# Turning the Fourier mixer's folded tokens by VectorE and DRAM instead of by TensorE

## The chip, the cores and the metric

The kernel runs on one core of a Trainium2 chip. The metric is the device time of one execution in microseconds (us); lower is better.

## What is computed

Three blocks follow each other on 2 batches of 3136 tokens with 256 features; all tensors are float32. The first is an attention with squared ReLU scores and a gate, the second a low-rank token mixer with an MLP, the third a Fourier mixer with a normalised MLP:

```python
out = u * (np.maximum(z @ z.T / S, 0.0) ** 2 @ v)      # attention, S = 3136
x   = out + (out.T @ U @ V).T                          # low-rank mixer
x   = x + np.maximum(x @ w_ch1, 0.0) @ w_ch2           # MLP, 256 -> 1024 -> 256
m   = np.real(fft(fft(x, axis=1), axis=2))             # Fourier mixer
y   = x + m
yn  = (y - mean(y)) / sqrt(var(y) + 1e-06)
res = y + np.maximum(yn @ w_ch1b, 0.0) @ w_ch2b        # second MLP
```

Matmuls take each float32 operand as a high and a low part (`h` and `l`, the low one being the value minus the high one), and do three products of four.

## The kernel before

**Stages.** Attention fills the first 549 us. Then 28 chunks of 448 tokens go through the two MLPs: 14 of layer 1 (7 for each batch), then 14 of layer 2. A chunk takes 8 steps, so that there are 224 steps, numbered here by the loop counter `i` of the last loop of `program` (lines 1091 to 1120). A plain step is 12 matmuls of 448 columns on TensorE (PE): six of `hidden(k)` for step i (L337 to L339) and six of `project` for step i-2 (L362 to L364). ScalarE (ACT) and VectorE (DVE) turn the hidden values into `Hh` (L342) and `Hl` (L343), which `project` needs two steps later.

**Work beside the steps.** After its 12 matmuls a step advances the generators in the list `active` by one piece each, and writes their instructions behind it on every engine. The newest chunk's preparation (`prep1`, `prep2`) stands first in the list, then the conversion of the second MLP's weights, then `fourier(b)`. Every engine executes its instructions in the order in which they were written. `fourier(0)` starts at step 50 and `fourier(1)` at step 106; both are skipped in steps whose number divides by 8 (56 and 112 here).

**The Fourier mixer's first half.** The mixer of a batch works on 8 groups of 4 x 98 tokens. Features come in pairs of halves that are folded: `fold(i)` adds them on DVE (L875, three sums, six for the first group) into a tile `y` with features on the partitions and 392 tokens in the free dimension. `tokens(i)` turns it token-major: four TensorE transposes of 98 tokens each (L886) into one PSUM bank, from which ACT makes `nh` (a copy, L93) and DVE `nl` (a difference, L96). `axis49(i)` applies the 49-point transform, three matmuls of 512 columns (L893 to L895), copies the result to `wst` on ACT and stores it into the DRAM tensor `scr` from SyncE (SP), L902. `pair_late()` hands out the pairs of `nh` and `nl`, of which there are two. In one step stand `fold(i)`, `tokens(i-1)` and `axis49(i-2)`, so that a group is folded in one step, turned in the next and transformed in the one after it. The two batches have 16 groups.

**After that** the mixer reads `scr` back (`fetch`, L938), applies the 64-point transform and the feature transform, and adds the result to `xT`.

**Queues.** `load` issues a DMA from SP, `late_dma` from GpSimd (POOL). SP issues in order: a DMA that waits for its data or its buffer holds up all that stand behind it. In the first half of the mixer SP's queue holds the stores into `scr` and a few of the weight conversion.

## Time and profile before

| | |
|---|---|
| time, median of 3 runs | 1165.17 us (1165.17 to 1165.97) |
| the profiled execution | 1166.43 us |
| its span, first to last instruction | 1164.7 us |
| PE busy | 1150.9 us (99%), 8438 matmuls |
| DVE busy | 853.5 us (73%) |
| ACT busy | 645.7 us (55%) |
| POOL busy | 141.7 us (12%) |
| TensorE clock granted, mean | 0.999 |
| DMA | 78.72 MB, 68 GB/s over the span |

Busy time counts an engine as busy while at least one of its instructions runs; matmuls overlap in the pipeline, so the length of a PE record (0.36 us for 448 columns) is longer than the distance from one start to the next. Distances between starts tell what an instruction costs.

### The profile page before, as it was taken

Reading aid. Unit: us, or ns where it says so; the run is one execution under the profiler, and the core shown is the slowest. Engines: PE = TensorE matmul, PEld = TensorE weight load, DVE = VectorE, ACT = ScalarE, POOL = GpSimd, SP = SyncE. Lnnn points to the kernel's source line nnn. Section 1 sums busy time; section 2 is a strip of 40 time slices with the busy share of each in tenths; the row PEclk is TensorE's granted clock in tenths of the full one; section 3 lists DMA queues with packets and bytes.
Section 4 is the critical chain, followed back from the end, with each engine's and each line's share of the span. In section 5 each row is a group of like instructions: output and inputs, shape, how many; then the busy total and the mean of one; then the engine's idle time right before and its main releaser. Section 6 shows DMA issues by size and latency. Waiting matters only on the chain.

```text
span 1164.7 us, 21602 instructions
## 1 busy us (share of the span) xinstructions
PE 1150.9 (99%) x8438; PEld 1075.7 (92%) x8438; DVE 853.5 (73%) x1599; ACT 645.7 (55%) x1061; POOL 141.7 (12%) x236
## 2 busy tenths in 40 slices
PE   9999999999999999999999999999999999999998
PEld 8999999999988999998999989999989999999997
DVE  6877888778888777777577674566487788767674
ACT  7867777777777666665354344333264443434342
POOL 0012320122012201220201000110000110000010
PEclk9999999999999999999999999999999999999999
DMA  4322222324222211221533322111012211110111
GB/s 140 95 59 63 77 86 61 97 74 129 68 53 92 73 40 57 74 78 43 172 98 118 107 86 75 28 33 55 1 46 69 49 48 40 32 40 26 40 32 48
DMA packets 64454, 78.72 MB, mean 68 GB/s; under 512 B 13150, under 2 KB 55008, under 8 KB 64352
## 3 DMA queue, kind: packets, MB, share of 16 engines
q1 hardware_dynamic: 53088, 56.98, 15.7%
q0 software_dynamic: 10848, 20.16, 6.7%
q8 instruction: 66, 1.08, 0.4%
q14 instruction: 36, 0.29, 0.1%
q10 hardware_dynamic: 416, 0.20, 0.1%
HBM read 51.89 MB, written 25.34 MB: 66 GB/s over the span
## 4 chain that ended last, share of the span: by engine, by line
PE 88%; DVE 7%; ACT 3%; issue 2%; DMA 1%; DVEq 0%; ACTq 0%; SPq 0%
PE psO L567 31%; PE psS L536 8%; PE psH L337 7%; PE psH L338 7%; PE psH L339 7%; PE psC L362 7%; PE psC L364 7%; PE psC L363 7%; DVE l L96 1%; ACT P L542 1%; ACT P L545 1%; DVE h L546 1%; DMA vraw<-in_v 1%; DVE Hl L343 1%; PE ps_g L840 1%
## 5 line engine op out<-in xcount | busy, mean ns | idle before, releaser
L567 PE MATMUL psO<-h,Vt 64*128 64x448 f32 x2744 | 347.4, 363 | 2.5 <-DVE h L546 1.5
L567 PEld LDWEIGHTS psO<-h,Vt 64*128 64x128 f32 x2744 | 294.5, 185 | 14.7 <-DVE h L546 2.6
L96 DVE TENSOR_TENSOR l<-P,h 128x896 fp32r<-128x896 f32 (+2 forms) x239 | 226.1, 951 | 33.7 <-ACT h L93 16.5
L343 DVE SCALAR_TENSOR_TENSOR Hl<-psH,Hh 128x448 fp32r<-128x448 f32 x224 | 139.0, 623 | 141.2 <-ACT Hh L342 139.9
L342 ACT ACTIVATE Hh<-psH 128x448 fp32r<-128x448 f32 x224 | 120.3, 541 | 203.9 <-PE psH L339 198.9
L567 PE MATMUL psO<-l,Vt 64*128 64x448 f32 x1372 | 209.5, 363 | 0.2
L542 ACT ACTIVATE P<-psS 128x896 f32<-128x896 f32 (+1 forms) x183 | 161.2, 882 | 66.5 <-PE psS L536 65.1
L545 ACT ACTIVATE P<-P 128x896 f32<-128x896 f32 (+1 forms) x183 | 168.5, 921 | 5.7
L337 PE MATMUL psH<-h,w 128*128 128x448 f32 x448 | 167.1, 373 | 0.0
L567 PEld LDWEIGHTS psO<-l,Vt 64*128 64x128 f32 x1372 | 161.4, 185 | 5.8 <-DVE l L96 1.2
L546 DVE CAST h<-P 128x896 fp32r<-128x896 f32 (+1 forms) x183 | 110.8, 606 | 75.4 <-ACT P L545 73.4
L338 PE MATMUL psH<-l,w 128*128 128x448 f32 x448 | 164.3, 367 | 0.0
L339 PE MATMUL psH<-h,w 128*128 128x448 f32 x448 | 163.9, 366 | 0.0
L362 PE MATMUL psC<-Hh,w 128*128 128x448 f32 x448 | 163.6, 365 | 0.0
L364 PE MATMUL psC<-Hh,w 128*128 128x448 f32 x448 | 163.4, 365 | 0.0
L363 PE MATMUL psC<-Hl,w 128*128 128x448 f32 x448 | 162.4, 362 | 0.0
L536 PE MATMUL psS<-Q,KT 64*128 64x448 f32 x1002 | 149.5, 364 | 3.6 <-DVE G L652 3.1
L536 PEld LDWEIGHTS psS<-Q,KT 64*128 64x128 f32 x1002 | 114.9, 185 | 8.7 <-DVE G L652 4.4
L337 PEld LDWEIGHTS psH<-h,w 128*128 128x128 f32 x448 | 84.3, 188 | 7.7 <-ACT P L93 0.3
L339 PEld LDWEIGHTS psH<-h,w 128*128 128x128 f32 x448 | 84.2, 188 | 7.2
L363 PEld LDWEIGHTS psC<-Hl,w 128*128 128x128 f32 x448 | 84.1, 188 | 7.1 <-DVE Hl L343 0.4
L364 PEld LDWEIGHTS psC<-Hh,w 128*128 128x128 f32 x448 | 84.1, 188 | 6.8
(302 smaller groups left out, 1201.1 us busy)
## 6 DMA issues: line engine op xcount, KB each, us to landing
uT<-in_uT SPq DMA_DIRECT2D x14, 448.0 KB, 3.9
vraw<-in_v SPq DMA_DIRECT2D x24, 256.0 KB, 2.8
out<-P SPq DMA_DIRECT2D x27, 224.0 KB, 1.9
aTd<-aT POOLq DMA_DIRECT2D x13, 448.0 KB, 2.9
aNd<-aT POOLq DMA_DIRECT2D x104, 56.0 KB, 2.4
xT<-aTd SPq DMA_DIRECT2D x6, 896.0 KB, 4.7
scr<-wst SPq DMA_DIRECT2D x16, 256.0 KB, 2.0
Vs<-Vd POOLq DMA_DIRECT2D x28, 112.0 KB, 2.5
```

The source lines that it names most:

```text
L96: tt(out=o, in0=a, in1=b, op=ALU.subtract)
L337: mm(ps[:, 0:CH], wh, self.h[:, a], start=a == 0, stop=False)
L338: mm(ps[:, 0:CH], wh, self.l[:, a], start=False, stop=False)
L339: mm(ps[:, 0:CH], wl, self.h[:, a], start=False, stop=a == 1)
L343: stt(out=l, in0=ps[:, 0:CH], scalar=0.0, in1=f(h), op0=ALU.max, op1=ALU.subtract)
L362: mm(dst, wh, h, start=k == 0, stop=False)
L363: mm(dst, wh, l, start=False, stop=False)
L364: mm(dst, wl, h, start=False, stop=k == 7)
L536: mm(ps[:, j, 0:w], k, q[r, kq, o : o + w], start=(kk, kq) == (0, 0), stop=kk == 1)
L542: act(out=dst, in_=ps[:, j : j + m, 0:w], func=AF.Relu, scale=1.0 / S)
L545: act(out=A[:, x], in_=A[:, x], func=AF.Square)
L567: mm(o[fa][i][:, 0:CH], vt[r, j, k, fa * 128 : fa * 128 + 128], x[r, j * CH : j * CH + CH], start=p == 0 and fa not in [t[1][0] for t in t ...
```

## The change

`fold(i)` now writes into one of two fixed tiles `ys`, padded from 392 to 416 tokens (13 blocks of 32; the padding is zeroed once by GpSimd). DVE turns it in blocks of 32x32 (`STREAM_TRANSPOSE`, L887), into a tile `yt` that shares its buffer with `A1` or `A2` of the mixer's second half. Each band of 32 features is then stored from SP into a new DRAM tensor `nat_d`, token-major, in pieces of 32 features (128 bytes): four DMAs of 52 KB a group (L889). `fetch_tokens(i)` reads 392 token rows of 128 features back from SP into the `nl` tile of a pair (196 KB, L896), and `tokens(i)` makes `nh` from it on ACT and `nl` in place on DVE. A third pair of `nh` and `nl` lies in the tile `Uhl`, which the low-rank mixer no longer needs then. In one step stand `fold(i)`, `fetch_tokens(i-2)`, `tokens(i-3)` and `axis49(i-4)`. The mixer's first half takes 12 pieces instead of 11 (ten, of which the first took two steps). The scratch tiles `sm` grow from four to five.

```diff
+    nat_d = [dram.tile([8, 416, 128], F32, tag=f"natd{b}", name=f"natd{b}") for b in range(NB)]
...
+    ys = [mp.tile([128, 416], F32, tag=f"y{k}", name=f"y{k}", bufs=1) for k in range(2)]
+    for t in (raw128, col128, *(f(r) for r in rows), *(y[:, 392:416] for y in ys)):
         nc.gpsimd.memset(t, 0.0)
...
-        for x in (*nats[0], *nats[1]):
+        uu = Uhl.rearrange("p k h n -> p (k h n)")
+        nats.append([uu[:, 0:512], uu[:, 512:1024]])
+        for x in (*nats[0], *nats[1], *nats[2]):
             nc.gpsimd.memset(f(x)[96:128], 0.0)
...
+            yt = mp.tile([128, 416], F32, tag=f"A{i % 2 + 1}", name="yt", bufs=1)
+            nc.vector.transpose(out=yt, in_=y)
+            for c in (0, 32, 64, 96):
+                load(
+                    out=nat_d[b][i, :, c : c + 32].rearrange("(j t) d -> t j d", t=32),
+                    in_=yt[c : c + 32].rearrange("p (j d) -> p j d", d=32),
+                )
+
+        def fetch_tokens(i):
+            h, l = nat[i] = pair_late()
+            load(
+                out=f(l)[0:98].rearrange("p (s d) -> p s d", s=4),
+                in_=nat_d[b][i, 0:392].rearrange("(s p) d -> p s d", p=98),
+            )
+
         def tokens(i):
-            y = folded.pop(i)
-            ps = misc()
-            for s in range(4):
-                nc.tensor.transpose(ps[0:98, s * 128 : s * 128 + 128], y[:, s * 98 : s * 98 + 98], ident)
-            h, l = pair_late()
-            hcopy(h[0:98], ps[0:98, :])
-            sub(l[0:98], ps[0:98, :], f(h[0:98]))
-            nat[i] = (h, l)
+            h, l = nat[i]
+            hcopy(h[0:98], f(l)[0:98])
+            sub(l[0:98], f(l)[0:98], f(h[0:98]))
...
-        for i in range(10):
+        for i in range(12):
             if i < 8:
                 fold(i)
-            if 0 < i < 9:
-                tokens(i - 1)
-            if i == 0:
-                yield
+            if 1 < i < 10:
+                fetch_tokens(i - 2)
+            if 2 < i < 11:
+                tokens(i - 3)
...
-            if i > 1:
-                axis49(i - 2)
+            if i > 3:
+                axis49(i - 4)
             yield
```

**On PE**, in `fourier(0)`, around the first transform (`ps_x`, `ps_g`, `ps_m` are PSUM banks, `psH` and `psC` those of the MLP). Before:

```order
L257 MATMUL ps_m<-Vs,Gs_87 128x448
L886 MATMUL ps_x<-ident,y 98x128 x4
L893 MATMUL ps_g<-nh_7998,b49h 128x512
L894 MATMUL ps_g<-nl_7999,b49h 128x512
L895 MATMUL ps_g<-nh_7998,b49l 128x512
L337 MATMUL psH<-h,w 128x448
```

and with the change, behind the last matmuls of `project` in step 54:

```order
L364 MATMUL psC_9281<-Hl,w 128x448
L365 MATMUL psC_9281<-Hh,w 128x448
L907 MATMUL ps_m<-nh_8004,b49h 128x512
L908 MATMUL ps_m<-nl_8005,b49h 128x512
L909 MATMUL ps_m<-nh_8004,b49l 128x512
L338 MATMUL psH<-h,w 128x448
```

The transposes are gone, and the first transform stands one step later than before, in step 54 instead of 53.

**On SP**, from the first store of `fourier(0)` on. Before:

```order
L902 DMA scr_70<-wst 128x512 x2
L1063 DMA w2bd<-Tl 128x256
L902 DMA scr_70<-wst 128x512 x3
L927 DMA raw_7988<-xT_7986 32x1x98
L902 DMA scr_70<-wst 128x512 x3
```

and with the change, from the first fold of `fourier(0)` on (`nl_8005`, `nl_8003` and `Uhl` are the three pairs' `nl`):

```order
L889 DMA natd_72<-yt 32x13x32 x12
L896 DMA nl_8005<-natd_72 98x4x128
L1077 DMA w2bd<-Th 128x256
L889 DMA natd_72<-yt 32x13x32 x4
L896 DMA nl_8003<-natd_72 98x4x128
L889 DMA natd_72<-yt 32x13x32 x4
L896 DMA Uhl<-natd_72 98x4x128
L916 DMA scr_70<-wst 128x512
```

Each read-back stands behind the four stores of the group that is folded in the same step: that of group 0 behind those of group 2.

**On DVE**, in `fourier(0)`, the end of step 52 and step 53. Before (`P` and `l` are of the chunk's preparation):

```order
L875 TENSOR_TENSOR y<-xT_7986 128x4x48 x2
L96 TENSOR_TENSOR nl_7999<-ps_g,nh_7998 98x512
L343 SCALAR_TENSOR_TENSOR Hl<-psH,Hh 128x448
L258 TENSOR_TENSOR P<-ps_m,xT_7987 128x448
L96 TENSOR_TENSOR l<-P,h 128x448
```

and with the change:

```order
L887 STREAM_TRANSPOSE yt<-y_7994 128x416
L344 SCALAR_TENSOR_TENSOR Hl<-psH,Hh 128x448
L259 TENSOR_TENSOR P<-ps_g,xT_7989 128x448
L96 TENSOR_TENSOR l<-P,h 128x448
L879 TENSOR_TENSOR y_7995<-xT_7988 128x4x2
L879 TENSOR_TENSOR y_7995<-xT_7988 128x4x48 x2
L887 STREAM_TRANSPOSE yt<-y_7995 128x416
L96 TENSOR_TENSOR nl_8005<-nl_8005,nh_8004 98x512
```

The turn of group 2 now ends the work of step 52, and the first `nl` stands in step 53, behind the fold and the turn of group 3.

## Rows read from the trace of the kernel before

**Rows 1.** The page, parts 1 and 4: busy time, and the chain's shares.

```profile
PE 1150.9 (99%) x8438; PEld 1075.7 (92%) x8438; DVE 853.5 (73%) x1599; ACT 645.7 (55%) x1061; POOL 141.7 (12%) x236
...
PE 88%; DVE 7%; ACT 3%; issue 2%; DMA 1%; DVEq 0%; ACTq 0%; SPq 0%
```

**Rows 2.** Line L886, the transposes: idle of their engine until y came (us, times).

```profile
  DVE y L875: 2.7, 3
```

**Rows 3.** Timeline of PE (start, length, instruction): step 57 and the next one's start.

```profile
700.91 0.36 PE L337 MATMUL psH<-h,w 128*128 128x448 f32 x1
...
703.34 0.60 PE L886 MATMUL ps_x<-ident,y 128*98 128x128 f32 x4
...
704.24 0.39 PE L895 MATMUL ps_g<-nh,b49l 128*128 128x512 f32 x1
704.47 0.36 PE L337 MATMUL psH<-h,w 128*128 128x448 f32 x1
```

**Rows 4.** Timeline of PE: starts of steps 52, 108, 113, 114, and late transposes in step 53.

```profile
682.86 0.37 PE L337 MATMUL psH<-h,w 128*128 128x448 f32 x1
...
689.80 0.64 PE L886 MATMUL ps_x<-ident,y 128*98 128x128 f32 x4 [1.04 <-DVE y L875]
...
845.58 0.37 PE L337 MATMUL psH<-h,w 128*128 128x448 f32 x1
...
861.79 0.36 PE L337 MATMUL psH<-h,w 128*128 128x448 f32 x1
...
865.56 0.36 PE L337 MATMUL psH<-h,w 128*128 128x448 f32 x1
```

**Rows 5.** Timeline of DVE: folds in steps 52, 57, 108, 113, 114, and neighbours.

```profile
689.05 0.69 DVE L875 TENSOR_TENSOR y<-xT 128x8 f32<-128x8 f32 x3
689.66 0.68 DVE L96 TENSOR_TENSOR nl<-ps_g,nh 98x512 fp32r<-98x512 f32 x1
...
704.50 0.70 DVE L875 TENSOR_TENSOR y<-xT 128x8 f32<-128x8 f32 x3
...
848.43 1.15 DVE L96 TENSOR_TENSOR P<-xT,ps_x 128x448 f32<-128x448 f32 x2 [0.15 <-PE ps_x L291]
...
849.83 0.70 DVE L875 TENSOR_TENSOR y<-xT 128x8 f32<-128x8 f32 x3
...
866.31 0.70 DVE L875 TENSOR_TENSOR y<-xT 128x8 f32<-128x8 f32 x3
...
871.59 0.70 DVE L875 TENSOR_TENSOR y<-xT 128x8 f32<-128x8 f32 x3
```

**Rows 6.** DVE's block turns there are: line L604 (nanoseconds), and the timeline.

```profile
L604 DVE STREAM_TRANSPOSE aT<-aT x13: 1103/1105/1111, 55.3 to 516.2; 128x896 f32<-128x896 f32 x13
...
729.68 0.20 DVE L916 STREAM_TRANSPOSE col<-wst 128x32 f32<-128x32 f32 x1
```

**Rows 7.** SP's timeline: four issues in a row; DMA view: KB each, us to landing.

```profile
737.02 1.71 SPq L938 DMA_DIRECT2D wr<-scr  x4
...
aNd<-aT POOLq DMA_DIRECT2D x104, 56.0 KB, 2.4
...
wst<-aNd SPq DMA_DIRECT2D x12, 256.0 KB, 2.7
...
wst<-aNd SPq DMA_DIRECT2D x1, 128.0 KB, 2.0
```

**Rows 8.** Timeline of ACT: the copy that makes nh.

```profile
703.97 0.59 ACT L93 CAST nh<-ps_x 98x512 fp32r<-98x512 f32 x1 [1.10 <-PE ps_x L886]
```

**Rows 9.** Windows: busy us of PE, PEld, DVE, ACT, POOL; clock; two fourier stretches, the end.

```profile
682.86:718.66 35.80, 34.76 (x181) 30.79 (x180) 23.53 (x57) 16.47 (x31) 1.28 (x3) 1.00 0.19 67
845.58:880.63 35.05, 34.57 (x180) 30.48 (x179) 29.72 (x79) 21.23 (x42) 1.10 (x2) 1.00 0.15 54
...
1160.00:1161.00 1.00, 0.19 (x1) 0.00 (x0) 1.00 (x4) 0.00 (x0) 0.00 (x0) 1.00 0.00 0
...
1163.00:1163.50 0.50, 0.00 (x0) 0.00 (x0) 0.00 (x0) 0.00 (x0) 0.00 (x0) 0.91 0.00 0
```

More of the change, by code (lines that the diff above doesn't have):

```diff
@@ L800, in program @@
     rows = [mp.tile([128, CH], F32R, tag=f"row{k}", name=f"row{k}", bufs=1) for k in range(2)]
-    for t in (raw128, col128, *(f(r) for r in rows)):
+    ys = [mp.tile([128, 416], F32, tag=f"y{k}", name=f"y{k}", bufs=1) for k in range(2)]
+    for t in (raw128, col128, *(f(r) for r in rows), *(y[:, 392:416] for y in ys)):
         nc.gpsimd.memset(t, 0.0)
     def small(dt=F32):
-        return mp.tile([128, CH], dt, tag="sm", name="sm", bufs=4)
+        return mp.tile([128, CH], dt, tag="sm", name="sm", bufs=5)
     late["small"] = small
@@ L854, in fourier @@
     def fourier(b):
-        folded, nat, W = {}, {}, {}
+        nat, W = {}, {}
         x0, x1 = (xT[b][:, a].rearrange("p (s m r) -> p s m r", m=49, r=2) for a in range(2))
         def fold(i):
-            y = folded[i] = mp.tile([128, 392], F32, tag="y", name="y")
+            y = ys[i % 2]
             s0, s1 = 4 * i, 4 * i + 4
-            yv = y.rearrange("p (s m r) -> p s m r", m=49, r=2)
+            yv = y[:, 0:392].rearrange("p (s m r) -> p s m r", m=49, r=2)
             for t0, t1 in ((0, 1), (1, s1)) if s0 == 0 else ((s0, s1),):
```

## The prediction

> **What bounds the kernel now.** First the page's busy times and the chain that ended last: PE is busy 99% of the span and holds 88% of the chain, DVE 7% [rows 1]. PE therefore sets the end, and a change is worth what it takes from PE's queue, less what it makes PE wait. Next the windows of the two stretches in which the mixer's first half runs, steps 52 to 61 and 108 to 117: in 35.8 and 35.1 us PE has no more than 1.0 and 0.5 us in which nothing runs, while DVE is busy 23.5 and 29.7 us [rows 9]. Then PE's timeline in one step. Step 57 starts at 700.91, its 12 matmuls fill 2.43 us, four transposes and three transform matmuls fill 1.13 us, and the next step starts at 704.47; a transform matmul takes 0.23 us from its start to the next one's [rows 3]. So a step is 2.43 us plain, 3.12 us with a transform (2.43 + 0.69), 3.56 us with the transposes too, and 0.20 us more where the preparation puts a matmul of 448 columns into it (a twelfth of 2.43). Last the waits at the transposes: PE's side stood idle 2.7 us in three places until DVE had folded y [rows 2], the longest 1.04 us in step 53 [rows 4]. The profiled execution took 1166.43 us, 1164.7 of span and 1.73 around it, which is 1.26 us (0.1%) above the median of the runs. I make the sum as a difference and put it on the median, 1165.17.
>
> **What goes from PE.** Four transposes cost 1.13 - 0.69 = 0.44 us of a step [rows 3]. There are 16 groups, so PE's queue loses 16 x 0.44 = 7.0 us. The waits for y go with them, up to 2.7 us [rows 2]. Gain 9.7 us, all on the path. The price of a transpose is settled by the row: 0.11 us each in this stream. The Trainium skill (VectorE: DVE Perf Modes, "The three transpose paths") gives TensorE 390 ns and VectorE 311 ns for a 128x128 block of 2-byte numbers, and its rules for kernel authors prefer TensorE where PSUM may be the destination. By that figure the 64 transposes would be worth 25 us and the gain 28; the pitch in the trace is less than a third of it, and the sum goes by the trace.
>
> **What is added to DVE.** One block turn a group. The trace has two sizes, 1.105 us for 896 columns and 0.20 us for 32 [rows 6]; the line through both gives 0.20 + 384 x 1.047 ns = 0.60 us for 416. Sixteen are 9.7 us, in stretches where DVE has 12.3 and 5.3 us free [rows 9]. As busy time they fit. The difference that makes nl reads SBUF instead of PSUM; I leave it at 0.68 us [rows 5], and the copy for nh at 0.59 us [rows 8]. The zeroing of padding and of Uhl is GpSimd's, which issues little then; the fifth sm tile costs nothing on any queue.
>
> **What is added to SP and where it leads.** A group now takes four stores and one read-back, five DMAs more in a step. Four issues in a row for 32 partitions each took 1.71 us [rows 7]. A read of 196 KB from DRAM lies between two rows, 2.0 us to landing for 128 KB and 2.7 us for 256 KB [rows 7]; I take 2.4. Bandwidth is no concern: DMA engines are busy 15 to 19% there [rows 9]. The order is. The program's order puts the read-back of group g-2 behind the four stores of group g, which wait for DVE's turn of group g, and DVE turns it at the end of what that step gives it. From the fold's start to the point where the transform has both halves of group g-2 the chain is: fold 0.61 (689.05 to 689.66) [rows 5], turn 0.60, four issues 1.71, landing 2.4, nh 0.59, nl 0.68, together 6.6 us. The transform stands on PE two steps after the fold's step, behind that step's 12 matmuls. It can start 0.23 us before nl is there, with the matmul that needs nh alone. With the lag from the start of a step on PE to its fold on DVE,
>
> PE's wait = lag + 6.6 - 0.23 - 2.43 - (the two steps) = lag + 3.94 - (the two steps).
>
> Behind the waiting transform stand the hidden matmuls of the next step, and so the whole of ACT's and DVE's work for it: nothing fills the gap. The lags, read from the trace of before:
>
> In fourier(0), step 52 starts at 682.86 [rows 4] and its fold at 689.05 [rows 5], because the preparation's copies and the weight conversion lie ahead of it. Lag 6.19. The two steps hold no transform yet, only 2.63 each. Wait 6.19 + 3.94 - 5.26 = 4.9 us in step 54. In step 57 a layer-1 chunk's end lies ahead of the fold: 704.50 - 700.91 = 3.59 [rows 3, 5], two steps of 3.12, wait 1.3 us in step 59. The groups between are covered by the first wait and by step 56, which the mixer skips; the last two read-backs stand behind no fold.
>
> In fourier(1), step 108 starts at 845.58 and the fold in it at 849.83 [rows 4, 5], lag 4.25. DVE is full there, with 0.15 us idle ahead of that row's preparation [rows 5], and the change puts a fold and two turns more ahead of it (0.61 + 1.20), so the lag becomes 5.9. The two steps take 2.63 and 2.43. Wait 4.8 us in step 110. Step 113: 866.31 - 861.79 = 4.52, steps of 3.32 and 3.12, wait 2.0 us. Step 114: 871.59 - 865.56 = 6.03, steps of 3.12 and 3.12 + 2.0, wait 1.7 us [rows 4, 5].
>
> Waits 4.9 + 1.3 + 4.8 + 2.0 + 1.7 = 14.7 us, against a gain of 9.7: plus 5.0 us.
>
> **The clock during the two long waits.** At the end of the program PE runs its last matmul at 1160.0 to 1160.2, and the granted clock, 1.00 until 1163.0, is 0.91 on average from there to 1163.5 [rows 9]: it falls from 2.4 to 1.2 GHz some three us after PE had nothing left. Two waits of almost 5 us lie within the reach of that. At the low level the matmuls take twice as long. No row shows a fall amid work, so I bound it: nothing if the clock stays, one whole step of 3.12 us more for each wait if it stays low over the step that follows. I take 1 us each, nearer to nothing, since PE had work until shortly before the clock could fall: plus 2.0 us. The Trainium skill (TensorE: Matmul & The Clock Gate, "Why this matters for your kernels") warns of idle gaps between bursts of matmuls, which bring the low level back; the end of this trace agrees with it, and by that rule the clock would fall in both waits, which is rival (c) below.
>
> Sum: 5.0 + 2.0 = 7.0 us, 1165.17 + 7.0 = 1172.2, and 1173.4 for an execution profiled as the one before. I predict 1172 us.
>
> **Bounds of the chain.** Low: landing 2.0, and stores issued in 0.3 us less, 5.9 in all, takes 0.7 from each of five waits, 3.5 us. High: landing 2.7, and the read-back held up behind the four stores in the same queue. Stores in pieces of 128 bytes are in the trace from GpSimd's queue alone, 2.4 us to landing for 56 KB [rows 7]; I allow 0.7 us for four from SP. That is 7.6 in all, 5 us more. With the clock at 0 to 6.2 us the forecast's mechanism spans plus 1.5 to plus 16 us, 1167 to 1181.
>
> **Rivals.** (a) The read-back is hidden and the 9.7 us are kept: 1155.5 us. For it speaks that DVE has the free time, and that the lag may shrink once DVE no longer stands behind copies from PE's transposes. Against it: in step 52 the budget from the fold to the transform is 2 x 2.63 + 2.43 + 0.23 - 6.19 = 1.7 us, less than the landing alone. It needs folds that start 5 us earlier than in the rows, or the first two waits to halve and the rest to vanish. (b) Only the first transform of each batch waits, with the short chain: 4.2 + 4.1 us against 9.7, and lesser waits of 1 or 2 us: about 1165, within 0.2%. For it: the later lags are read from a kernel in which PE itself waited. (c) The clock falls in both long waits and stays low for a step or more, on top of stores that hold up the read-back: 1176 to 1181. It decides if the clock falls within the waits as it did at the end of the program [rows 9]. That the change leaves transposes in the queue is no case: none of L886 stands in the new order of PE.
>
> **How the numbers follow.** Forecast 1167.5 to 1176: 0.46. Rival (c), 1176 to 1181 and a little beyond: 0.22. Rival (b), 1163 to 1167.5: 0.17. Rival (a) and its parts, 1155 to 1163: 0.15. About 0.2% (2.3 us) is what a measurement of this kernel tells from no change, so slower 0.68, same 0.17, faster 0.15. The range leaves out most of (a) and the far end of (c): 1161 to 1181.
>
> **What the changed profile would show.** Right: line L886 gone; L907 or L908 with an idle time of 4 to 5 us before it near 690 us and again near 851 us, released by ACT's nh or DVE's nl, and on ACT the nh copies waiting for a DMA into nl; SP's read-backs starting some 1.7 us after the first store of the same step; L887 at about 0.60 us; steps 55 to 61 without waits near 3.12 us. Wrong: PE's first transform with a wait below 2 us, which would mean that the folds come earlier than in the rows; a read-back that lands within 1.5 us; or PE's steps between the waits longer than 3.12 us, which would point at the clock or at Hh and Hl coming late.

## The result, and the profile after the change

The changed kernel takes 1180.64 us (median of 4 runs, 1179.66 to 1181.75) against 1165.56 us before (1165.17 to 1165.97): a ratio of 1.0129, with a 95% interval of 1.0113 to 1.0144. It is slower by 15.1 us; the forecast was 7.0. The sign was right, the size was not. The profiled execution took 1181.75 us, with a span of 1180.0.

The page after the change: part 1, the row of the clock from part 2, and the lines of part 4 (compare [rows 1]):

```profile
PE 1151.9 (98%) x8374; PEld 1064.3 (90%) x8374; DVE 863.8 (73%) x1615; ACT 645.3 (55%) x1061; POOL 143.0 (12%) x240
...
PEclk9999999999999999999999989999989999999999
...
PE psO L568 30%; PE psS L537 8%; PE psH L338 7%; PE psH L340 7%; PE psH L339 7%; PE psC L363 7%; PE psC L364 7%; PE psC L365 7%; DVE l L96 1%; DVE h L547 1%; ACT P L546 1%; ACT P L543 1%; DMA nl<-natd 1%; DMA zraw<-in_zT 1%; SPq L889 1%
```

PE has 64 instructions fewer and is busy 1.0 us longer. Two slices of the clock's row fall below 9, which are the two Fourier stretches, and the chain that ended last now runs through the read-back (`DMA nl<-natd`) and the four stores (`SPq L889`).

The timeline of PE shows what the transform waits for. Below are the instructions with a wait in front of them (in brackets: idle us, and what ended it), and a few behind the first:

```profile
695.56 0.79 PE L907 MATMUL ps_m<-nh,b49h 128*128 128x512 f32 x1 [5.27 <-ACT nh L93]
...
697.30 0.57 PE L338 MATMUL psH<-h,w 128*128 128x448 f32 x1
697.68 0.57 PE L339 MATMUL psH<-l,w 128*128 128x448 f32 x1
...
702.00 0.36 PE L338 MATMUL psH<-h,w 128*128 128x448 f32 x1
702.21 0.36 PE L339 MATMUL psH<-l,w 128*128 128x448 f32 x1
...
711.03 0.50 PE L908 MATMUL ps_m<-nl,b49h 128*128 128x512 f32 x1 [0.38 <-DVE nl L96]
715.93 0.50 PE L907 MATMUL ps_x<-nh,b49h 128*128 128x512 f32 x1 [1.75 <-ACT nh L93]
...
865.52 0.80 PE L907 MATMUL ps_m<-nh,b49h 128*128 128x512 f32 x1 [4.83 <-ACT nh L93]
...
881.00 0.50 PE L907 MATMUL ps_x<-nh,b49h 128*128 128x512 f32 x1 [0.39 <-ACT nh L93]
...
886.20 0.50 PE L907 MATMUL ps_g<-nh,b49h 128*128 128x512 f32 x1 [1.32 <-ACT nh L93]
...
891.13 0.49 PE L907 MATMUL ps_x<-Uhl,b49h 128*128 128x512 f32 x1 [0.84 <-ACT Uhl L93]
...
910.30 0.28 PE L907 MATMUL ps_m<-Uhl,b49h 128*128 128x32 f32 x1 [1.16 <-ACT Uhl L93]
```

These are steps 54, 58, 59, 110, 114, 115, 116 and 122. In steps 59 and 114 to 116 the transform's second matmul then waits for `nl` for 0.22 or 0.23 us more. Together PE stands 16.8 us in front of the transforms. The matmuls of step 55 (from 697.30) follow each other every 0.38 us, those from 702.00 every 0.21: the windows of the three stretches in which that is so show the lower level of the clock (columns as in [rows 9], the granted clock is the third last):

```profile
695.50:701.00 5.50, 5.44 (x14) 4.39 (x15) 4.79 (x12) 2.10 (x5) 0.00 (x0) 0.53 0.40 77
717.50:721.50 4.00, 4.00 (x14) 3.54 (x13) 1.32 (x2) 1.55 (x3) 0.00 (x0) 0.57 0.73 216
865.50:871.50 6.00, 5.98 (x15) 4.87 (x16) 5.21 (x11) 4.15 (x9) 0.00 (x0) 0.51 0.36 70
```

With work on PE throughout, 5.5 x 0.47 + 4.0 x 0.43 + 6.0 x 0.49 = 7.2 us of PE's time went there. What left PE's timeline is 7.0 us of transposes and 1.3 us of waits for `y`: 1.04 in step 53 [rows 4] and this one in step 115 of the kernel before:

```profile
872.44 0.61 PE L886 MATMUL ps_g<-ident,y 128*98 128x128 f32 x4 [0.23 <-DVE y L875]
```

Waits of 16.8 and a clock worth 7.2, less these 8.3, make 15.7 us; the span grew by 15.3. That is where PE's time went. What each part is worth when it alone is taken away is another matter, and the experiments answer that.

The first wait, step by step, in the timelines of DVE, SP and ACT: group 2's fold and turn, the read-back of group 0 behind group 2's four stores (these end the row of 12 stores), and ACT's copy for `nh`:

```profile
688.56 0.70 DVE L879 TENSOR_TENSOR y<-xT 128x8 f32<-128x8 f32 x3
689.29 0.61 DVE L887 STREAM_TRANSPOSE yt<-y 128x416 f32<-128x416 f32 x1
...
682.08 9.75 SPq L889 DMA_DIRECT2D natd<-yt  x12
691.93 0.42 SPq L896 DMA_DIRECT2D nl<-natd  x1
...
694.89 0.62 ACT L93 CAST nh<-nl 98x512 fp32r<-98x512 f32 x1 [2.54 <-DMA nl<-natd]
```

From the turn's end (689.90) to the read-back's issue 2.0 us, from there to ACT's copy 3.0.

### The profile page after: what moved, and what is told of

Its sections match the earlier page's. It is cut to its first block, busy times and chain, and to the rows that moved or that the text cites. A ratio compares the mean times of both kernels' runs of the same rounds, so it can differ in the third digit from the quotient of the medians.

```text
span 1180.0 us, 21635 instructions
## 1 busy us (share of the span) xinstructions
PE 1151.9 (98%) x8374; PEld 1064.3 (90%) x8374; DVE 863.8 (73%) x1615; ACT 645.3 (55%) x1061; POOL 143.0 (12%) x240
## 4 chain that ended last, share of the span: by engine, by line
PE 86%; DVE 6%; ACT 3%; DMA 2%; issue 2%; SPq 1%; DVEq 0%; ACTq 0%
PE psO L568 30%; PE psS L537 8%; PE psH L338 7%; PE psH L340 7%; PE psH L339 7%; PE psC L363 7%; PE psC L364 7%; PE psC L365 7%; DVE l L96 1%; DVE h L547 1%; ACT P L546 1%; ACT P L543 1%; DMA nl<-natd 1%; DMA zraw<-in_zT 1%; SPq L889 1%
## 5 line engine op out<-in xcount | busy, mean ns | idle before, releaser
L568 PEld LDWEIGHTS psO<-h,Vt 64*128 64x128 f32 x2744 | 289.7, 184 | 18.9 <-DVE h L547 2.6
L568 PEld LDWEIGHTS psO<-l,Vt 64*128 64x128 f32 x1372 | 158.9, 184 | 8.8 <-DVE l L96 1.6
L339 PEld LDWEIGHTS psH<-l,w 128*128 128x128 f32 x448 | 85.0, 190 | 6.6
```

Of the source, the lines that this page charges most:

```text
L339: mm(ps[:, 0:CH], wh, self.l[:, a], start=False, stop=False)
L568: mm(o[fa][i][:, 0:CH], vt[r, j, k, fa * 128 : fa * 128 + 128], x[r, j * CH : j * CH + CH], start=p == 0 and fa not in [t[1][0] for t in t ...
```

## The experiments

Times are medians; "plus" and "minus" are against the median of the kernel before in the same comparison (1165.24 to 1165.65), and differences between two kernels are differences of these. Step numbers are those of the kernel before, as in the prediction. A difference of two of these kernels is uncertain by one to two us, as the intervals show. In the runs on ready data, without turn, without round trip and without transposes the transform works on other data than the kernel's own.

| kernel | us | ratio to before, 95% interval |
|---|---|---|
| the change | 1180.64 | 1.0129 (1.0113 to 1.0144) |
| read-back first | 1170.57 | 1.0048 (1.0031 to 1.0065) |
| ready data, all work kept | 1169.68 | 1.0033 (1.0022 to 1.0044) |
| first waits filled with matmuls | 1181.05 | 1.0127 (1.0111 to 1.0144) |
| no turn at all | 1162.21 | 0.9966 (0.9953 to 0.9979) |
| read-back first, one step more | 1164.57 | 0.9991 (0.9982 to 1.0000) |
| read-back and nh/nl first | 1175.74 | 1.0090 (1.0075 to 1.0105) |
| turn, no round trip | 1167.99 | 1.0023 (1.0012 to 1.0033) |
| nh/nl first, one step more | 1172.01 | 1.0061 (1.0044 to 1.0077) |
| before, no transposes | 1161.59 | 0.9967 (0.9954 to 0.9980) |
| turn, no round trip, waits filled | 1165.91 | 1.0006 (0.9996 to 1.0015) |
| turn, no round trip, folds on GpSimd | 1165.15 | 0.9996 (0.9987 to 1.0006) |
| one step more, folds on GpSimd | 1162.82 | 0.9978 (0.9969 to 0.9988) |
| before, folds on GpSimd | 1166.30 | 1.0008 (0.9999 to 1.0018) |
| one step more, GpSimd, column early | 1162.07 | 0.9971 (0.9962 to 0.9981) |

**Read-back first.** The changed kernel, with two calls swapped:

```diff
-            if i < 8:
-                fold(i)
             if 1 < i < 10:
                 fetch_tokens(i - 2)
+            if i < 8:
+                fold(i)
```

> Only the order within a step changes: the read-back of group g-2 is written ahead of group g's fold, turn and four stores. Theory (PE waits for the read-back because SP issues it behind the same step's turn and four stores): the fold (0.7 us), the turn (0.6 us) and the four issues (1.9 us) leave the chain, the data lies in nl some 3 us sooner, and no copy for nh waits for a DMA any more. DVE still makes the difference for nl behind the next group's fold and turn (that ended at 693.46 in the changed kernel, nl at 696.2), so about 2 us of each long wait goes, not all: 1170 to 1176 us. Rival A (the landing time or the 128-byte-wide stores themselves are the delay): same time as the changed kernel, 1180. Rival B (SP's order is the whole wait): the waits vanish, 1164 to 1168.

Measured: 1170.57, plus 5.1, which is 10.0 us less than the changed kernel, at the edge of what the theory gave, and neither rival's time. In SP's timeline group 0's read-back now stands ahead of group 2's stores, and ACT's copy for group 0's `nh` waits for nothing; but PE's first transforms still wait:

```profile
685.89 0.34 SPq L896 DMA_DIRECT2D nl<-natd  x1
689.54 1.91 SPq L889 DMA_DIRECT2D natd<-yt  x4
...
691.86 0.60 ACT L93 CAST nh<-nl 98x512 fp32r<-98x512 f32 x1
...
692.52 0.79 PE L907 MATMUL ps_m<-nh,b49h 128*128 128x512 f32 x1 [2.62 <-ACT nh L93]
...
856.83 0.80 PE L907 MATMUL ps_m<-nh,b49h 128*128 128x512 f32 x1 [2.60 <-ACT nh L93]
```

So the order on SP's queue was worth 10 us, two thirds of the loss, though the two long waits shrank by less than half: from 5.27 to 3.0 us (2.62, and 0.38 for `nl`) and from 4.83 to 2.6. What is left of them is work of the preparation and the weight conversion on ACT and DVE, which stands ahead of `nh` and `nl`; the run with turns and no round trip, below, waits as long. (Later copies for `nh` still wait for their read-back, as the one at 885.35, 4.84 us.) Part of the 10 us goes with the clock. The changed kernel's four executions all had a mean granted clock of 0.992 or 0.993. Of this kernel's five only the profiled one did, with three falls, and it took 1174.77, some 6 us less than the changed kernel; the other four, at 0.996 to 0.999, took 1169.5 to 1171.4. What is left, 5.1 us above the kernel before, is not SP's order.

**Ready data.** Every turn, store and read-back stays, but the read-backs fill columns that nobody reads:

```diff
 def fetch_tokens(i):
-    h, l = nat[i] = pair_late()
+    k = i % 2 * 512
     load(
-        out=f(l)[0:98].rearrange("p (s d) -> p s d", s=4),
+        out=f(uu)[0:98, k : k + 512].rearrange("p (s d) -> p s d", s=4),
...
 def tokens(i):
-    h, l = nat[i]
-    hcopy(h[0:98], f(l)[0:98])
-    sub(l[0:98], f(l)[0:98], f(h[0:98]))
+    h, l = nat[i] = pair_late()
+    r = f(uu)[0:98, 1024:1536]
+    hcopy(h[0:98], r)
+    sub(l[0:98], r, f(h[0:98]))
```

> All the work of the changed kernel is kept (turns, stores, read-backs), but the read-backs go into spare columns that nobody reads, and the copy and difference for nh and nl read 98x512 numbers that have been ready for long. What is left out: the transform works on other data, so nobody waits for the round trip. Theory (the wait is the loss, the added work lies beside PE's): both long waits and the falls of the clock in the two stretches vanish, 1155 to 1159 us. Rival (the added DVE turns, SP issues or DMA packets slow the stretches by themselves): 1165 to 1180.

Measured: 1169.68. My theory falls, the rival holds: with no read-back to wait for, the kernel is still 4.2 us slower than before, and within the intervals as fast as with the read-back first. Once the read-back is early, waiting for it costs no more than 0.9 us by the medians; something else in the added work costs the rest.

**No turn at all.** The same, without the turn, the stores and the read-backs (`tokens` as in the run above, `fetch_tokens` not called):

```diff
-            yt = mp.tile([128, 416], F32, tag=f"A{i % 2 + 1}", name="yt", bufs=1)
-            nc.vector.transpose(out=yt, in_=y)
-            for c in (0, 32, 64, 96):
-                load(
...
```

> As the run on ready data, with the turns, stores and read-backs left out too: neither TensorE nor VectorE turns the tokens, the folds stay, and nh and nl are made from numbers that are ready (so the transform works on other data). What PE's transposes and the waits for y are worth: theory 9.7 us below the kernel before, 1155.5 us (1154 to 1157). If the run on ready data with the turns kept takes the same time within 1 us, the added work of DVE, SP and the DMA engines costs nothing by itself. Rival (the slots of the transposes are partly idle time that PE would spend waiting for ACT or DVE anyway): 1160 or more.

Measured: 1162.21, minus 3.2 and not 9.7: the rival holds. The gain that the forecast put first does not exist in that size. This is not the price of the transposes alone: in the changed order PE still waits 2.0 and 0.3 us in step 54, behind work of the preparation and the weight conversion on ACT and DVE, and 1.2 us for the 128th column's small transform in step 122.

**Turn, no round trip.** It splits the 7.5 us between the last two: the turn stays, the stores and read-backs go.

```diff
             nc.vector.transpose(out=yt, in_=y)
-            for c in (0, 32, 64, 96):
-                load(
...
```

> As the run on ready data, with DVE's turns kept and the stores and read-backs left out (nobody reads the turned tiles, the transform works on other data). It splits the 7.5 us between the run without any turning (1162.2) and the run with turns, stores and read-backs that nobody waits for (1169.7). Theory (DVE's 0.61 us a group ahead of the difference for nl, and the clock that falls in the longer wait): 1168 to 1170. Rival (SP's issues and the 98599 DMA packets): 1162 to 1164.

Measured: 1167.99, plus 2.3. This is the lower end of the theory. The turn on DVE, 16 times 0.61 us, is worth 5.6 us by itself, with the falls of the clock that its waits bring; SP's issues and the DMA packets add 1.9 us, which the intervals do not tell from nothing (plus 4.2 against plus 2.3). The windows of the second stretch, from the start of step 108 to that of step 118, without the turn and with it (columns: PE, PEld, DVE, ACT, POOL busy, clock, DMA share, GB/s):

```profile
843.49:876.31 32.82, 31.01 (x146) 26.61 (x144) 28.70 (x78) 20.22 (x41) 1.12 (x2) 1.00 0.14 49
```

```profile
844.98:883.49 38.51, 33.63 (x146) 29.00 (x145) 33.34 (x86) 20.50 (x41) 1.11 (x2) 0.91 0.12 42
```

Without the transposes PE has 31.0 us of work there. DVE has 28.7 without the turns and 33.3 with them: more than PE. But the stretch grew from 32.8 to 38.5 us, and a DVE with 33.3 us of work bounds it at 33.3 only. In PE's books 2.6 of these 5.7 us are the same work at a lower clock (0.91 on average), and 3.1 are waits. In the first transform of batch 0 PE waits for `nh`, and in that of batch 1 for `nl`, which stands behind DVE's preparation, fold and turn:

```profile
691.60 0.79 PE L899 MATMUL ps_m<-nh,b49h 128*128 128x512 f32 x1 [2.62 <-ACT nh L93]
...
855.81 0.79 PE L900 MATMUL ps_m<-nl,b49h 128*128 128x512 f32 x1 [2.94 <-DVE nl L96]
```

**Before, no transposes.** The gain term alone, in the order and with the lags of the kernel before:

```diff
-            y = folded.pop(i)
-            ps = misc()
-            for s in range(4):
-                nc.tensor.transpose(ps[0:98, s * 128 : s * 128 + 128], y[:, s * 98 : s * 98 + 98], ident)
+            folded.pop(i)
             h, l = pair_late()
-            hcopy(h[0:98], ps[0:98, :])
-            sub(l[0:98], ps[0:98, :], f(h[0:98]))
+            r = f(Uhl.rearrange("p k h n -> p (k h n)"))[0:98, 1024:1536]
+            hcopy(h[0:98], r)
+            sub(l[0:98], r, f(h[0:98]))
```

> The kernel before, in its own order and with its own lags, with the 64 transposes left out: nh and nl are made from numbers that are ready, so the transform works on other data, and the folds are computed and not read. This is the gain term of the forecast alone. Theory of the forecast (four transposes a group lie on the path, 0.44 us each group, and the waits for y go with them): 9.7 us less, 1155 to 1157. Rival (DVE and ACT need nearly the whole of these steps themselves, so part of the transposes' time on PE turns into waiting): 1159.5 to 1163.

Measured: 1161.59, minus 3.9, as the rival had it. The timeline of PE shows waits in place of the transposes:

```profile
689.61 0.50 PE L892 MATMUL ps_m<-nl,b49h 128*128 128x512 f32 x1 [1.84 <-DVE nl L96]
...
860.90 0.36 PE L337 MATMUL psH<-h,w 128*128 128x448 f32 x1
...
863.92 0.51 PE L891 MATMUL ps_g<-nh,b49h 128*128 128x512 f32 x1 [0.43 <-ACT nh L93]
865.21 0.36 PE L337 MATMUL psH<-h,w 128*128 128x448 f32 x1
...
868.83 0.50 PE L892 MATMUL ps_m<-nl,b49h 128*128 128x512 f32 x1 [0.80 <-DVE nl L96]
869.40 0.37 PE L337 MATMUL psH<-h,w 128*128 128x448 f32 x1
```

In step 53 the wait for `y` of 1.04 us [rows 4] became one for `nl` of 1.84. Step 114 runs here from 860.90 to 865.21, 4.31 us without transposes; in the kernel before it took 4.07 with them, from 865.56 [rows 4] to

```profile
869.63 0.36 PE L337 MATMUL psH<-h,w 128*128 128x448 f32 x1
```

Step 115 takes 4.19 us here (to 869.40) and took 4.12. All in all PE's waits in the two stretches, 1.5 us in the kernel before, are 3.8 us here. In such steps the preparation's work on DVE and ACT sets the length, and the transposes ran in time that PE had to wait anyway.

**First waits filled.** The changed kernel, with matmuls in the wait:

```diff
 def axis49(i):
     ps = misc()
+    for _ in range(18 if i == 0 else 0):
+        mm(ps, b49h, uu[:, 1024:1536], start=True, stop=True)
     dft49(ps, *nat.pop(i))
```

> The changed kernel with 18 spare matmuls of 512 columns ahead of the first transform of each batch (some 4.1 us at 0.23 us each), into the PSUM tile that the transform then overwrites: PE is busy for most of the 5.3 us wait. Theory (the clock falls because PE runs empty, and the matmuls after the wait run at half speed for 5 us): the two low stretches near 694 and 865 vanish, steps 55 and 111 take about 3.2 us and not 4.7 and 5.0, and the time falls by about 5 us, to 1175 to 1177. Rival (the steps after the wait are long because ACT, DVE or the next read-back are late): the clock may stay up, but the time stays at 1180, or rises by what the spare matmuls overrun.

Measured: 1181.05, no change. PE's timeline in steps 54 and 55:

```profile
688.95 4.29 PE L915 MATMUL ps_m<-Uhl,b49h 128*128 128x512 f32 x18
694.52 0.49 PE L908 MATMUL ps_m<-nh,b49h 128*128 128x512 f32 x1 [1.29 <-ACT nh L93]
...
695.82 0.36 PE L338 MATMUL psH<-h,w 128*128 128x448 f32 x1
...
699.72 0.50 PE L908 MATMUL ps_x<-nh,b49h 128*128 128x512 f32 x1 [1.33 <-ACT nh L93]
...
702.00 0.57 PE L340 MATMUL psH<-h,w 128*128 128x448 f32 x1
```

The clock stayed up through step 54 (0.36 us matmuls at 695.82), but step 55 now met a wait for the next read-back, of which the changed kernel had none, and there the clock fell (0.57 us at 702.00). In the second batch, too, the fall moved, to behind a wait of 2.65 us at 885.49. The four executions had a mean granted clock of 0.995 or 0.996, against 0.992 or 0.993 in the changed kernel, and were no faster. So this run doesn't show what the clock alone costs. It shows that time won right behind the first wait is lost again at the next read-back.

**Turn, no round trip, waits filled.** Where no read-back follows, the clock can be priced:

```diff
+            for _ in range((10, 14)[b] if i == 0 else 0):
+                mm(ps, b49h, uu[:, 1024:1536], start=True, stop=True)
             dft49(ps, *nat.pop(i))
```

> As the run with turns and no trip, with 10 spare matmuls of 512 columns ahead of the first transform of the first batch and 14 in the second (2.3 and 3.2 us, less than the waits there of 2.6 and 3.0 us). It prices the clock where no read-back is late behind the wait. Theory (the fall costs what the doubled matmuls add: step 55 took 4.99 instead of 3.12, step 111 5.41 instead of 3.34, and about 0.5 us in each waiting transform): 1163 to 1165. Rival (DVE's work for the next steps ends no sooner, so PE waits for it instead): 1167 to 1169.

Measured: 1165.91, plus 0.4, which is 1.9 us less than without the filling (the intervals just overlap), and between theory and rival. Windows of the profiled executions, without the filling and then with it:

```profile
691.50:698.50 7.00, 6.51 (x17) 5.28 (x18) 6.17 (x17) 2.63 (x6) 0.00 (x0) 0.53 0.17 59
855.50:862.00 6.50, 6.19 (x16) 5.38 (x17) 5.55 (x13) 3.33 (x7) 0.00 (x0) 0.50 0.11 40
```

```profile
690.00:695.00 5.00, 4.00 (x17) 2.79 (x16) 4.31 (x11) 3.23 (x7) 0.00 (x0) 1.00 0.09 26
...
855.00:860.00 5.00, 5.00 (x25) 4.24 (x24) 4.66 (x12) 3.73 (x8) 0.00 (x0) 1.00 0.14 52
```

The two falls took 6.5 x 0.47 + 6.2 x 0.50 = 6.2 us of PE's busy time. But the 1.9 us is not simply their price, since not every execution without the filling had both: the profiled one (1169.39, mean granted clock 0.993) is the slowest of eight, and three at 0.997 to 0.999 took 1167.3 to 1167.7. Within this kernel, then, two falls go with some 2 us, about 1 us a fall. The filled kernel (0.999 or 1.0 throughout) is one to two us faster than those three as well, and why is not shown. DVE was busy 6.17 of 7.00 and 5.55 of 6.50 us in the windows of the falls, so a faster PE had little to gain there.

**Turn, no round trip, folds on GpSimd.** One word in `fold`:

```diff
-                    tt(
+                    nc.gpsimd.tensor_tensor(
```

> As the run with turns and no trip, with the folds on GpSimd instead of DVE: DVE's work in a group is then about what it was without the turn (0.69 us of folds go, 0.61 of turn stay). Theory (DVE's work in these steps is the bound that the turn hits): 1161.5 to 1164, as without any turning. Rival (it is not DVE's sum but the place of the turn ahead of nl, or the folds on GpSimd come so late that the turn holds DVE up): 1167 or more.

Measured: 1165.15, minus 0.3, which is 2.7 us less than with the folds on DVE: half of the turn's 5.6 us comes back when DVE's load goes back to about what it was. Less than the theory had, and less than the rival feared. The turn still stands ahead of `nl`, and in two places it waited for GpSimd's `y`, 4.3 us in all; which of the two keeps the other half was not tested.

**Read-back first, one step more.** The transform a step later, with a seventh half-tile for `nl`:

```diff
+        hs = [p[0] for p in nats]
+        ls = [*(p[1] for p in nats), uu[:, 1024:1536]]
...
-            h, l = nat[i] = pair_late()
+            h, l = nat[i] = hs[i % 3], ls[i % 4]
...
-        for i in range(12):
+        for i in range(13):
...
-            if i > 3:
-                axis49(i - 4)
+            if i > 4:
+                axis49(i - 5)
```

> The read-back written ahead of the fold, and each group's transform one step later on PE (three steps behind the read-back instead of two; a seventh half-tile for nl in spare columns makes that possible). Theory now (with the read-back early, PE still waits 4.3 us in step 54 and 3.8 us in step 110 for nh and nl, because ACT and DVE take their work in order and stand a step behind the preparation's chain): one step more of 2.4 to 3.1 us covers most of it, no fall of the clock, 1157 to 1164 us, at or below the kernel before. Rival (DVE has too much work for these steps, and its backlog delays Hl and so the hidden layer's own matmuls wherever the transform stands): the waits only move one step, 1167 to 1172.

Measured: 1164.57, minus 1.1, which is 6.2 us less than with the read-back first alone, and as fast as the kernel before, 0.6 us above the theory's range. The first transform of batch 0 now waits 0.2 and 0.7 us. In its place `project` waits, 1.41 us in step 58 and 2.06 us in step 114, for DVE's addition into `xT`, and around the second of these DVE is busy 14.96 of 15.20 us (third and fourth row: PE's timeline, and a window with columns as above):

```profile
693.07 0.50 PE L910 MATMUL ps_m<-nh,b49h 128*128 128x512 f32 x1 [0.18 <-ACT nh L93]
694.25 0.50 PE L911 MATMUL ps_m<-nl,b49h 128*128 128x512 f32 x1 [0.68 <-DVE nl L96]
...
863.70 0.44 PE L363 MATMUL psC<-Hh,w 128*128 128x448 f32 x1 [2.06 <-DVE xT L373]
...
851.00:866.20 15.20, 12.63 (x56) 10.60 (x55) 14.96 (x37) 8.04 (x18) 0.28 (x1) 0.94 0.63 130
```

Here the rival is right in kind, though not in size: DVE's backlog is what PE meets next.

**Read-back and nh/nl first**, and the same with one step more: `tokens(i - 3)` too is written ahead of `fold(i)`.

```diff
             if 1 < i < 10:
                 fetch_tokens(i - 2)
+            if 2 < i < 11:
+                tokens(i - 3)
             if i < 8:
                 fold(i)
-            if 2 < i < 11:
-                tokens(i - 3)
```

> As the run with the read-back first, and the copy and difference for nh and nl also ahead of the next group's fold and turn. Theory (nl comes late because DVE does a fold and a turn, 1.3 us, ahead of the difference): the transform's second matmul starts up to 1 us sooner in each wait, 1167 to 1169.5 us. Rival (DVE is the bound in these steps, so what is put ahead comes back behind it): 1170 to 1172, as the run with the read-back first.

> Read-back and the nh/nl step ahead of the fold, and the transform one step later. If both orders matter: 1156 to 1161 us, below the kernel before. If the step more is enough by itself: as the run with one step more. If DVE's backlog decides: 1167 to 1171.

Measured: 1175.74 and 1172.01, 5.0 and 7.4 us more than their counterparts, and worse than every theory had it. In the first of them the first wait shrank by 0.16 us only, from 3.00 to 2.84. DVE now stands before the difference until the read-back has landed, and `Hl` and the folds behind it with it; and the last read-backs are late, as here in step 117 (timelines of DVE and ACT):

```profile
886.64 0.69 DVE L96 TENSOR_TENSOR nl<-nl,nh 98x512 fp32r<-98x512 f32 x1 [2.60 <-ACT nh L93]
...
886.00 0.62 ACT L93 CAST nh<-nl 98x512 fp32r<-98x512 f32 x1 [4.56 <-DMA nl<-natd]
```

No run took this wait away by itself, so that it makes up the whole 5 us is not shown.

**One step more, folds on GpSimd**, and its control, the kernel before with the same word changed:

> The run with one step more (read-back first, transform a step later), with the folds on GpSimd: the complete computation. Theory (what is left there is DVE's load): 1158 to 1162, below the kernel before by more than 0.2%. Rival (GpSimd's folds take so long that turn, stores and read-back move back by more than DVE gains): 1165 or more.

> The kernel before with the folds on GpSimd and nothing else changed. Theory (VectorE already sets the pace of steps 53, 114 and 115 in the kernel before, where leaving the transposes out won nothing): the waits there shrink, 1162.5 to 1164.5 us. Rival A (TensorE alone sets the pace before, VectorE's 0.62 us a group is free there): 1165 to 1166. Rival B (GpSimd's slower folds make the transposes wait for y): 1167 or more.

Measured: 1162.82, minus 2.7, between theory and rival; and 1166.30, plus 1.1, which the interval does not tell from no difference. Neither theory's time came; the control is nearest to its rival A. So GpSimd's folds win nothing as long as TensorE turns the tokens, and the first kernel is not faster than before by its folds alone. Against the run with one step more and folds on DVE they win 1.6 us by the medians, with intervals that overlap. In the second stretch DVE there has 25.4 us of work in 31.6 (first row; same columns as above), although GpSimd takes 725 ns for a sum of 128x192 (second row: busy us, mean ns):

```profile
841.59:873.19 31.60, 29.82 (x143) 26.12 (x141) 25.37 (x49) 16.54 (x34) 10.01 (x19) 1.00 0.56 110
...
L882 POOL TENSOR_TENSOR y<-xT 128x192 f32<-128x192 f32 x28 | 19.7, 725 | 6.2 <-DVE xT L373 6.2
```

In the control the transposes of one step waited for GpSimd's `y` instead, so that a gain on DVE may be hidden behind it:

```profile
868.33 0.64 PE L886 MATMUL ps_m<-ident,y 128*98 128x128 f32 x4 [1.27 <-POOL y L875]
```

**The 128th column early.** Last, the small transform that waited 1.16 us in step 122 of the changed kernel is moved into the loop (it takes its `h` and `l` from `hs` and `ls`):

```diff
...
                 axis49(i - 5)
+            if i == 11:
+                col = column128()
+            if i > 10:
+                next(col)
             yield
...
-        yield from column128()
-        for _ in range(2):
+        for _ in range(3):
             yield
```

> The run with one step more and the folds on GpSimd, with the transpose and transform of the 128th column put into two steps of the loop that hold no preparation, ahead of the place where they stood. Theory (the 2.3 us lost at step 123 are the wait of that small transform for its copies on ACT and DVE): 1160 to 1161.5. Rival (the preparation's chain is late there anyway): 1162.5 to 1163.5.

Measured: 1162.07, neither theory's time nor the rival's, and not told apart from 1162.82 by the intervals. Its ten executions fall in two groups: three with a mean granted clock of 0.998 took 1163.5 to 1163.7, and seven at 0.999 or 1.0 took 1159.5 to 1162.8. The profiled one is of the first group, and in it the clock falls behind a wait of 1.36 us for this very transform, at 883.04. It and the run ahead of it are the fastest complete kernels of this study, 0.3% and 0.2% below the kernel before.

## Why the forecast was right in sign and half in size

The runs give this ledger, each line the difference of two medians, good to one or two us: without transposes in the changed order minus 3.2; DVE's turns plus 5.6; stores and read-backs that nobody waits for plus 1.9, and waiting for an early read-back plus 0.9, neither told from nothing; the read-back behind the stores plus 10.0. The sum is 15.2; the lines run from the kernel before to the changed one, so they add up by construction, and each holds in this order of steps only. Against it, the forecast had minus 9.7 for the first line, nothing for the second, and 16.7 for the waits and the clock, where the ledger has 12.8. Two steps failed, then: the gain, 6.5 us too large, and DVE's turns, 5.6 us put at nothing. The trip through DRAM, 3.9 us too dear, hid part of that.

**What bounds the kernel: right, but only half read.** PE's timeline was full in both stretches [rows 9], and I took a full engine for the only one that counts. Moving the folds away from DVE changed nothing in the kernel before, which fits that PE set the pace in most steps there, though GpSimd's later `y` may have hidden a gain; and it was with little to spare, since DVE's free time in the second stretch was 5.3 us.

**What goes from PE: the step that failed first.** "Gain 9.7 us, all on the path." Taken away alone, the transposes gave 3.9 us. The duration of 0.11 us each stands. One part was a misreading: of the 2.7 us in [rows 2], 1.3 are PE's own waits and 1.4 are the weight loads' (PEld), which stood idle over the same time in step 53:

```profile
689.79 0.39 PEld L886 LDWEIGHTS ps_x<-ident,y 128*98 128x98 f32 x4 [1.42 <-DVE y L875]
```

So the rows gave 8.3 us, not 9.7, and the sum would have come to plus 8.4. The other part is that a step does not get shorter by what PE loses: steps 114 and 115 are no shorter without transposes, and the waits for `y` turned into longer waits for `nl`. The Trainium skill (VectorE: DVE Perf Modes, "The three transpose paths"), by whose 390 ns the gain would have been an estimated 28 us, is further off still; measured in the kernel, 64 transposes are worth 3.9 us, about 60 ns each.

**What is added to DVE: size right, verdict wrong.** The turn took 0.61 us, forecast 0.60. But "as busy time they fit" put its cost at nothing, and the runs showed 5.6 us. It compared 9.7 us of turns with the free time of a stretch that the change itself makes shorter. The sum to make was: the second stretch's 29.72 us of DVE [rows 9] and eight turns of 0.61 are 34.6; PE's 34.57 less eight times 0.44 are 31.1. DVE becomes the longer one; the run with turns and no round trip showed 33.3 us of DVE, against 31.0 of PE without the turns. That sum is only part of the 5.6 us: the stretch took 38.5 us in that run. The turn also stands ahead of `nl` in DVE's order, and with the folds moved away half of the 5.6 us stayed.

**SP's chain: right as the chain that ended last, not as the only one.** The lag of step 52 was 6.19 us as forecast (688.56 - 682.37, the step's start in the trace after), four stores took 1.9 to 2.0 us instead of 1.71, the first read-back 3.0 us to ACT's copy instead of 2.4. The long waits came as 5.27 and 4.83 us, forecast 4.9 and 4.8; steps 59, 115 and 116 as 2.0, 1.6 and 1.1, forecast 1.3, 2.0 and 1.7. Waits of 0.4, 0.6 and 1.2 us in steps 58, 114 and 122 were not foreseen. In all 16.8 against 14.7. The run that swapped two calls shows the order on SP as the cause of only part of the long waits: 3.0 and 2.6 us of them stay, and 3.0 and 2.9 us with no round trip at all. A second chain, the work of the preparation and the weight conversion on ACT and DVE ahead of `nh` and `nl`, ended some 2 us before SP's, and the forecast had no such chain. That the long waits came out so near was in this sense luck.

**The clock: mis-sized in PE's books, about right in price.** I allowed two falls at 1 us each. It fell three times and took 7.2 us of PE's time; the third fall came behind the wait of 1.75 us in step 59. In PE's books this is the largest miss: 5.2 us, beside 2.1 of waits and the 1.4 counted twice. Priced by whole executions of the kernel with turns and no trip, two falls go with some 2 us, which is the 1 us each. In the changed kernel filling the first waits won nothing, because the forecast's "the groups between are covered by the first wait" holds only while PE is slow: with the clock up, step 55 waits for the next read-back. The term I lacked is this next wait. The Trainium skill (TensorE: Matmul & The Clock Gate, "Why this matters for your kernels") says that idle gaps between bursts of matmuls bring the low level back; the trace agrees, with three falls, each behind a wait. The two runs with filled waits show that a fall costs less than the slow matmuls suggest when another engine is next in line.

**The rivals.** Rival (c), 1176 to 1181, is what the time came to; I gave it 0.22. Its clock fell as it said, and the first trip, 5.0 us from the turn's end to ACT's copy where the forecast's chain had 4.1, came near the upper bound. But it kept the gain of 9.7 us and the free turns, so that its time is in part luck. Rival (a), the trip hidden, needs more than a better order: with the read-back first and a step more the time only reaches that of the kernel before, since DVE is then in the way.

What stays open: the two ways of reckoning, PE's books (waits 16.8, clock 7.2, gain 8.3) and the ledger of runs (gain 3.2, the rest 18.4), describe the same 15 us and can't be mixed. Of the 10 us of the read-back's place, about 6 remain when executions of equal granted clock are compared, but that rests on a single execution. Nor is it shown why the order with `nh` and `nl` first costs 5 us.

## What to carry to other kernels

When work leaves the engine that bounds a stretch, make the sum of every engine anew for the shorter stretch, with the added work in it: here DVE's 33 us overtook PE's 31, and a gain forecast at 9.7 us was 3 to 4 before any cost. Then look where in that engine's order the work stands, since the sum alone explained only part of the 5.6 us. A load that was due long ago must not stand on an in-order queue behind stores that wait for this step's result; swapping two calls was worth 10 us here. Ask, too, which chain would end last if that one were gone: with the read-back out of the way, over half of the long waits stayed. And a wait's price is found by taking it away alone, not by adding up idle time and slow matmuls, which cover for each other.

## What the runs showed of the hardware

The granted clock fell to the lower level amid work, which no row of before had shown, and not only behind the waits of 5 us: also right behind the 1.75 us wait of step 59. The same kernel's executions differed in it: with turns and no trip, mean granted clocks of 0.993 to 0.999 and times of 1167.3 to 1169.4 us. Two falls took 6.2 us of PE's busy time there and went with some 2 us of the kernel's. A read-back of 196 KB that SP issued at 691.93, right behind its four stores of 52 KB, took 3.0 us to the first use. A sum of 128x192 on GpSimd took 725 ns on average, and DVE's block turn of 128x416 took 593 to 615 ns in all runs.
